# Pinning TensorE's whole order: attention steps placed by counted MLP columns, scores in one burst over four banks, full-height transposes

## The chip, the cores and the metric

The kernel runs on one core of one Trainium2 chip. The core has five engines with instruction queues of their own: TensorE (PE, matrix products), VectorE (DVE), ScalarE (ACT), GpSimd (POOL) and SyncE (SP, which issues most DMAs). The metric is the device time of one launch in microseconds (us), as the median of several runs.

## What is computed

Windowed attention with a linear bias for 8 batches of 8 heads, then a gated MLP on its output. Cut to what matters (here `B, H, S, D = 8, 8, 576, 64`, `d_model` 512, `d_ff` 1024):

```python
scores = q @ k.T / sqrt(D)                       # per batch and head
mask = (rel >= 0) & (rel < 128)                  # rel = query - key position
scores = where(mask, scores - slope[h] * abs(rel), -1e9)
attn = softmax(scores);  x = attn @ v            # heads side by side: [B, S, 512]
h = gelu_tanh(x @ w_in);  u, v = h[..., :512], h[..., 512:]
v_n = (v - mean(v)) / sqrt(var(v) + 1e-6) * g_ln
v_s = einsum('ts,bsd->btd', w_sg, v_n) + b_sg[None, :, None]
out = x + (u * v_s) @ w_out
```

## The kernel before

Attention is done for pairs of heads: 32 pairs, four to a batch, pair n in batch n // 4. A pair goes through steps with one-letter names (the table `STEPS`). Queries and keys come transposed, so that the window of 128 keys is met by blocks of 64 queries against 192 keys. The scores of a pair come in two parts, `a` (`scores(0)`, 12 matmuls with the first block's short ones) and `c` (`scores(2)`, 8 matmuls), each into two banks of PSUM of the pool ps_s, which has two. VectorE adds the bias and takes the minima of the negated scores (`A`, `C`), which also writes the tiles `e` and `e0` to SBUF and so frees the banks; `n` copies the minima to `nb`. ScalarE takes the exponentials (`E`, eight 128x128 tiles and two 64x64 of `e0`, L363), VectorE the inverses of the sums (`R`), and GpSimd scales (`r`, `s`, `S`). PE transposes the four tiles of a head (`t`, `T`, L388) and the small first block (`z`, L401: a 64-row `e0` against a 64x64 identity) into banks of ps_a, which also has two; VectorE masks them on the way out into `px` (`X`, `Y`), ScalarE copies the small block into `p0` (`P`, L404). The step `v` multiplies with the values: one matmul `x2` from `p0` (L421) and 18 into `x1` from `px` (L418). ScalarE gathers both into `xf` (`x`), and `h`, `l`, `k` split it for the MLP into a high and a low half `xs`.

The MLP of a batch (`mlp_block`) runs in parts: a tail of v (L517, L519), two v parts of two 128-row tiles (`v_sum`, L489 to L491, 12 matmuls of 512 columns for each tile), four u parts (L466 to L468, 24 matmuls of 288 columns), four y parts (L551 to L555, 28 of 288 columns) and four output parts (L466 to L468 again, 24 of 288). fp32 is carried as high and low halves, so that three matmuls stand for one product. Each part fills one of the two double banks of ps_m; ScalarE's gelu (L509, L524) and the norm, which goes over VectorE, GpSimd and ScalarE and back, follow a v part, and the results `vn`, `vA`, `vB` are read by y.

The order. The first five pairs are written out by hand in the string `START`, on all engines, with the decoding of the 64-bit weights between; tokens are a step and a pair (`v4`), and `w` tokens are v_sums of the first batch. From the sixth pair on (`FIRST = 5`) the code is issued by a small plan (`PLAN`, `PLAN0`): digits advance a pair to a stage of `STAGES`, letters the pair before, and `m` emits the next MLP part whole. That fixes dependencies and priorities; the order on each engine is then made by the scheduler, which works with modelled times. `burst` keeps the matmuls of a step one behind the other as far as `issue_after` holds them.

A "tail" below is the v tail of a batch, from its L517. There is one in each batch.

Of the kernel before, what the change touches and what calls it, by code (L numbers as in the profile page):

```python
# [21 lines left out]
def attention_gmlp(  # L22
# [17 lines left out]
    nc = tc.nc  # L40
# [244 lines left out]
    class Pair:  # L285
# [25 lines left out]
        def scores(self, t2):  # L311
            qk, heads = self.qk, self.heads
            W = 3 * R
            if t2 == 0:
                self.pr = [att.tile([P, T, P], F32, name="e", bufs=4) for _ in range(2)]
                self.e0 = att.tile([R, 2 * R], F32, name="e0", bufs=2)
            banks = self.banks[t2] = [ps_s.tile([P, 512], F32, name="ps_s") for _ in range(2)]
# [17 lines left out]
            burst(insts)  # L335
# [5 lines left out]
        def minima(self, t2):  # L341
            W = 3 * R
            banks, pr, nm = self.banks.pop(t2), self.pr, self.nm
            for j in range(2):
# [6 lines left out]
                if t2 == 0:  # L351
                    self.shift(h, self.e0[:, j * R:(j + 1) * R], banks[j][0:R, 2 * W:2 * W + R], biases[h][0:R, 2, :], nm[0:R, 2 * T + j:2 * T + j + 1])
# [7 lines left out]
        def exps(self, ts, first=True):  # L360
            def exp(x, i):
                n = x.shape[0]
                nc.scalar.activation(x, x, AF.Exp, bias=self.nm[0:n, i:i + 1], scale=-1.0, accum_out=self.sm[0:n, i:i + 1])  # L363

            for j in range(2):
                for t in ts:
                    exp(self.pr[j][:, t, :], j * T + t)
            for j in range(2 if first else 0):
                exp(self.e0[:, j * R:(j + 1) * R], 2 * T + j)
# [10 lines left out]
        def scale_first(self):  # L380
            self.scaled(self.e0.rearrange("p (m c) -> p m c", m=2), 2 * T)
# [17 lines left out]
        def transpose_first(self):  # L399
            self.ct0 = ps_a.tile([P, 512], F32, name="ps_a")  # L400
            nc.tensor.transpose(self.ct0[:, 0:R], self.e0, ident[0:R, 0:R])  # L401
# [4 lines left out]
        def values(self):  # L406
            vt, px, heads = self.vt, self.px, self.heads
            x1 = self.x1 = ps_a.tile([P, 512], F32, name="ps_a")
            x2 = self.x2 = ps_a.tile([P, 512], F32, name="ps_a")
# [11 lines left out]
            burst([lambda: nc.tensor.matmul(x2[:, 0:R], self.vd, self.p0, start=True, stop=True), *(part(half, t, j) for half, t in order for j in (1, 0))])  # L421
# [18 lines left out]
        def low_tail(self):  # L440
# [11 lines left out]
            "T": lambda p: p.transpose(1), "Y": lambda p: p.masked(1), "v": values, "x": gather, "h": high, "l": low, "k": low_tail,  # L452
        }
        STAGES = ["qL", "aA", "cC", "n", "ER", "rstXzP", "STY", "vx", "hlk"]


    def mm3(dsts, pairs, outer=True):
        if not outer:
            for k in range(len(dsts)):
                mm3(dsts[k:k + 1], [(a, bs[k:k + 1]) for a, bs in pairs])  # L460
            return
# [31 lines left out]
    def v_sums(t2, xs):  # L493
        pv = ps_m.tile([P, 2, 512], F32, name="ps_m")
        for i in range(2):
            v_sum(pv, t2, i, xs, range(NC))
        return pv

    def mlp_block(b, xs, xfs):
# [6 lines left out]
        def v_part(t2):  # L506
            pv = started.pop(t2) if b == 0 and t2 in started else v_sums(t2, xs)
            vg = mlp.tile([P, 2, F], F32, name="vg", bufs=1)
            nc.scalar.activation(vg, pv, AF.Gelu_apprx_tanh)  # L509
            for i in range(2):  # L510
                norm(vg[:, i, :], P, vn[:, 0, t2 + i, :], vn[:, 1, t2 + i, :])

        def v_tail():
# [11 lines left out]
            norm(vg, R, vA[0:R], vA[R:2 * R], vB[0:R])  # L525

        def u_part(f):
            fs = slice(f * P, (f + 1) * P)
            pu = ps_m.tile([P, 2, 512], F32, name="ps_m")
            mm3([pu[:, i, 0:S2] for i in range(2)], [((wi[:, 0, c, fs], wi[:, 1, c, fs]), [(hi_of(xs[c])[:, ss], lo_of(xs[c])[:, ss]) for ss in halves]) for c in range(NC)], U_OUTER)  # L530
            nc.scalar.copy(in2(u4[:, f, :]), pu[:, :, 0:S2])
            us.append(u4[:, f, :])
            if f == NF - 1:
                nc.scalar.activation(u4, u4, AF.Gelu_apprx_tanh)

# [3 lines left out]
        for part, i in FIRST_ORDER if b == 0 else IN_ORDER:  # L539
            {"v": v_part, "t": lambda _: v_tail(), "u": u_part}[part](i)  # L540
            yield
        for f in range(NF):
# [5 lines left out]
            for i, ss in enumerate(halves):  # L548
# [6 lines left out]
                nc.tensor.matmul(y, vB[:, fs], wsB[:, ss], start=False, stop=True)  # L555
            nc.vector.tensor_tensor(in2(u), py[:, :, 0:S2], in2(u), ALU.mult)
            split(g[:, 0, :], g[:, 1, :], u)
            yield
        for c in range(NC):
# [3 lines left out]
            mm3([po[:, i, 0:S2] for i in range(2)], [((wo[:, 0, f, cs], wo[:, 1, f, cs]), [(gs[f][:, 0, ss], gs[f][:, 1, ss]) for ss in halves]) for f in range(NF)], O_OUTER)  # L563
            nc.vector.tensor_tensor(in2(o), po[:, :, 0:S2], in2(o), ALU.add)  # L564
            nc.sync.dma_start(out[b, cs, :], o)
            yield
# [3 lines left out]
    U_OUTER = 0  # L570
    O_OUTER = 1
    LAG = 2
# [7 lines left out]
    done = [0] * len(pairs)  # L580
    mlps = (b for b in range(B) for _ in mlp_block(b, xss[b], xfs[b]))
    parts = 0
# [7 lines left out]
        e1 r0 i5 s0 C1 z0 t0 S0 q3 +0 X0 a2 H1 i3 P0 -1 d5 T0 Y0 i4 -2 H0 f1 A2 v0 -0 L2 x0 R1 c2 m5 e2 r1 b5  # L590
        z1 C2 s1 q4 S1 t1 X1 a3 P1 f2 o5 T1 +5 Y1 h0 R2 d4 v1 A3 s2 l0 x1 L3 H5 t2 m4 k0 w10 b4 e3 X2 -5 w20
        c3 o4 w00 r2 C3 +4 z2 w30 P2 h1 S2 f3 a4 l1 T2 Y2 w31 H4 R3 k1 v2 -4 d3 A4 w01 r3 L4 x2 s3 w11 h2 m3
        t3 S3 e4 z3 X3 w21 l2 c4 T3 b3 w02 o3 k2 w32 Y3 P3 +3 d6 w12 C4 v3 H3 i7 -3 w22 x3 m6 h3 b6 f4 l3 o6
        w13 k3 +6 R4 w23 d7 w03 r4 H6 w33 m7 s4 z4 P4 b7 t4 S4 X4 -6 T4 o7 Y4 +7 v4 H7 -7 x4 h4 l4 k4
# [3 lines left out]
    wchunks = {}  # L598

# [14 lines left out]
    for token in START.split():  # L614
        before = len(nc.cur_bb.bb.instructions)
        start_step(token[0], int(token[1:]))
        for i in nc.cur_bb.bb.instructions[before:]:
            if i.engine in last:
                tc.add_manual_dep(i, last[i.engine], mybir.DependencyInfo(mybir.DependencyClass.NoSync, mybir.DependencyReason.DATA), reason="start")
            last[i.engine] = i.name  # L620
    for n in range(FIRST):
        done[n] = len(Pair.STAGES)

# [3 lines left out]
    PLAN = ['L1fmmg2hm34mi', '1mm2gh3m4Lm5i', 'def1Lgmmmhm2i', 'def1gmmhiLm2m']  # L627
    PLAN0 = {5: '1mLm2m34', 6: 'f1mgL2hm34mi', 7: 'f1mgL2hm34mi', 8: 'f1mgL2hm34mi', 9: '1mm2gh3m4Lm5i'}

    def advance(n, stage):  # L630
        if 0 <= n < len(pairs):
            while done[n] <= stage:
                for op in Pair.STAGES[done[n]]:
                    Pair.STEPS[op](pairs[n])
                done[n] += 1

    nc.sync.dma_start(gb, g_ln.rearrange("(o f) -> o f", o=1).broadcast_to([P, F]))
    steps = decode()
    vec.steps = steps
    for n in range(FIRST, len(pairs) + 1):  # L640
        advance(n, 0)
        for op in PLAN0[n] if n in PLAN0 else PLAN[n % NPAIR]:
            if op == "m":
                if parts < max((n - LAG) // NPAIR, 1) * (len(IN_ORDER) + NF + NC):
                    next(mlps)
                    parts += 1
            elif op == "L":
                advance(n + 1, 0)
            elif op.isdigit():
                advance(n, int(op))  # L650
            else:
                advance(n - 1, ord(op) - ord("a"))
        if n == LAST:
            vec.steps = None
            for _ in steps:
                pass
    for _ in mlps:
        pass
# [25 lines left out]
```

## Time and profile before

| what | us |
|---|---|
| median of three runs | 677.32 |
| lowest and highest | 675.35, 680.73 |
| the profiled execution | 675.89 |
| its span (first to last instruction) | 674.2 |

The granted clock of TensorE was .983 of full speed over the profiled span. A row of the order of time has the start in us, the duration, the engine, the line, the operation, the tiles it writes and reads, the shape and how many records it joins; in square brackets how long the engine idled before, and what ended that. An fp32 matmul leaves two records, so that the 12 score matmuls of the first part read `x24` and the 8 of the second `x16`. PE's durations overlap, since its matmuls are pipelined: what one costs is read from the starts of two that follow each other, not from its own duration.

### The profile page before, as it was taken

The numbers are of one execution on the slowest core, as the hardware profiler recorded it, in microseconds if no ns is written. First come the engines' busy times: TensorE is split into PE (matmuls) and PEld (weight loads), VectorE is DVE, ScalarE is ACT, GpSimd is POOL, SyncE is SP. The second block draws the span as 40 slices with busy tenths as digits, with TensorE's granted clock in tenths as the row PEclk, the third lists the DMA queues.
The fourth block names the chain that finished last, engine by engine and source line by source line (L and its number), as shares of the span: only waits on it lengthen the run. The fifth ranks groups of instructions, "written<-read, shape, count | busy, mean of one in ns | idle before, by whom it ended". The sixth has DMA issues, their size and how long they took to land.

```text
span 674.2 us, 14921 instructions
## 1 busy us (share of the span) xinstructions
PE 638.0 (95%) x5664; PEld 562.6 (83%) x5664; DVE 417.2 (62%) x1372; ACT 334.1 (50%) x979; POOL 244.2 (36%) x241
## 2 busy tenths in 40 slices
PE   3788796999999999999999999999999999999997
PEld 2666585887898889888899889889799888999997
DVE  5887996556646665655576656646576657553511
ACT  7676776434574326633645336742645345731420
POOL 1786657332134322551324321453226321360120
PEclk9998797999999999999999999999999999999999
DMA  8648330233212312224122322133221331001001
GB/s 273 209 128 241 114 125 8 74 106 111 72 48 80 112 53 73 73 74 143 57 59 69 107 73 73 41 103 116 69 59 56 108 106 36 1 2 71 0 1 71
DMA packets 55931, 57.24 MB, mean 85 GB/s; under 512 B 8498, under 2 KB 45362, under 8 KB 55860
## 3 DMA queue, kind: packets, MB, share of 16 engines
q1 hardware_dynamic: 55860, 56.28, 26.7%
q8 instruction: 45, 0.74, 0.5%
q14 instruction: 26, 0.21, 0.1%
HBM read 46.83 MB, written 9.44 MB: 83 GB/s over the span
## 4 chain that ended last, share of the span: by engine, by line
PE 75%; DVE 13%; ACT 7%; DMA 2%; issue 2%; POOL 1%; ACTq 0%; DVEq 0%; POOLq 0%
PE ps_m L466 9%; PE ps_m L467 8%; PE ps_m L468 8%; PE ps_s L320 7%; PE ps_a L418 7%; PE ps_m L551 5%; PE ps_m L552 5%; PE ps_m L553 5%; PE ps_a L388 4%; PE ps_m L489 3%; PE ps_m L490 3%; PE ps_m L491 3%; ACT e L363 3%; DVE vn L482 2%; DVE px L260 2%; DVE st L474 2%
## 5 line engine op out<-in xcount | busy, mean ns | idle before, releaser
L378 POOL TENSOR_TENSOR e<-e,rr 128x512 f32<-128x512 f32 (+1 forms) x96 | 77.9, 833 | 170.7 <-DVE rr L260 140.9
L363 ACT ACTIVATE e<-e,nb 128x128 f32<-128x128 f32 x270 | 101.7, 378 | 28.8 <-DVE nb L260 28.7
L320 PE MATMUL ps_s<-qk 64*64 64x192 f32 (+2 forms) x1280 | 79.7, 326 | 12.3 <-DMA qk<-qkT 8.0
L466 PE MATMUL ps_m<-xs,wi 128*128 128x288 f32 x256 | 79.2, 309 | 0.9 <-ACT vg L509 0.5
L551 PE MATMUL ps_m<-ws,vn 128*128 128x288 f32 x256 | 79.1, 309 | 0.0
L466 PE MATMUL ps_m<-g,wo 128*128 128x288 f32 x256 | 77.9, 305 | 0.2 <-DVE xf L564 0.2
L477 POOL TENSOR_TENSOR rs<-rs,mhalf 128x1 f32<-128x1 f32 (+1 forms) x40 | 35.3, 893 | 116.2 <-DVE rs L476 116.2
L552 PE MATMUL ps_m<-ws,vn 128*128 128x288 f32 x256 | 77.1, 301 | 0.0
L468 PE MATMUL ps_m<-xs,wi 128*128 128x288 f32 x256 | 76.9, 300 | 0.0
L553 PE MATMUL ps_m<-ws,vn 128*128 128x288 f32 x256 | 76.8, 300 | 0.0
L467 PE MATMUL ps_m<-g,wo 128*128 128x288 f32 x256 | 76.7, 301 | 0.0
L467 PE MATMUL ps_m<-xs,wi 128*128 128x288 f32 x256 | 76.6, 299 | 0.0
L320 PEld LDWEIGHTS ps_s<-qk 64*64 64x64 f32 x1280 | 50.2, 141 | 31.0 <-issue 18.9
L468 PE MATMUL ps_m<-g,wo 128*128 128x288 f32 x256 | 75.7, 297 | 0.0
L251 POOL TENSOR_TENSOR g<-u,g 128x576 fp32r<-128x576 f32 x32 | 45.4, 1419 | 68.3 <-ACT g L250 62.8
L418 PE MATMUL ps_a<-px,vt 128*64 128x128 f32 (+1 forms) x1152 | 64.4, 267 | 4.6 <-issue 2.8
L418 PEld LDWEIGHTS ps_a<-px,vt 128*64 128x64 f32 x1152 | 59.3, 142 | 10.3 <-issue 8.9
L260 DVE CUSTOM_DVE_ANT_0 e<-ps_s,bias 128x128 f32<-128x128 f32 (+1 forms) x256 | 57.1, 265 | 0.4
L260 DVE TENSOR_TENSOR px<-ps_a,m_old 128x512 f32<-128x512 f32 x64 | 43.8, 685 | 19.8 <-PE ps_a L388 19.5
L489 PE MATMUL ps_m<-wi,xs 128*128 128x512 f32 x128 | 52.5, 410 | 2.4 <-ACT xs L433 2.4
L438 POOL TENSOR_TENSOR xs<-xf,xs 128x576 fp32r<-128x576 f32 x32 | 46.4, 1461 | 21.1 <-DVE xs L260 20.9
L551 PEld LDWEIGHTS ps_m<-ws,vn 128*128 128x128 f32 x256 | 49.2, 192 | 3.7 <-issue 2.2
(113 smaller groups left out, 1487.6 us busy)
## 6 DMA issues: line engine op xcount, KB each, us to landing
qk<-qkT SPq DMA_DIRECT2D x32, 576.0 KB, 3.9
vt<-v_in SPq DMA_DIRECT2D x64, 256.0 KB, 3.2
outT<-xf SPq DMA_DIRECT2D x32, 288.0 KB, 2.1
wst<-w_in SPq DMA_DIRECT2D x8, 512.0 KB, 7.2
vt<-v_in SPq DMA_DIRECT2D x64, 32.0 KB, 2.9
wst<-w_out SPq DMA_DIRECT2D x4, 512.0 KB, 3.9
wst<-w_sgT SPq DMA_DIRECT2D x4, 288.0 KB, 4.1
vd<-v_in SPq DMA_DIRECT2D x64, 16.0 KB, 2.1
```

Source lines behind the costliest of these rows:

```text
L260: inst = getattr(nc.vector, name)(*args, **kw)
L320: return lambda: nc.tensor.matmul(dst, qk[js, 0, q0:q0 + R], qk[js, 1, k0:k1], start=True, stop=True)
L363: nc.scalar.activation(x, x, AF.Exp, bias=self.nm[0:n, i:i + 1], scale=-1.0, accum_out=self.sm[0:n, i:i + 1])
L378: nc.gpsimd.tensor_tensor(x, x, self.rr[0:n, i:i + m].rearrange("p (m o) -> p m o", o=1).broadcast_to([n, m, c]), ALU.mult)
L418: return lambda: nc.tensor.matmul(x1[heads[j], q0 + lo // 2 * R if t < 0 else q0 + t * R:q0 + (hi + 1) // 2 * R], block, px[j][:, (half * ...
L466: nc.tensor.matmul(dst, ah, bh, start=(i == 0), stop=False)
L467: nc.tensor.matmul(dst, ah, bl, start=False, stop=False)
L468: nc.tensor.matmul(dst, al, bh, start=False, stop=(i == n - 1))
L489: nc.tensor.matmul(pv[:, i, :], xh, wi[:, 0, c, F:], start=(c == 0), stop=False)
L551: nc.tensor.matmul(y, vn[:, 0, t, fs], ws[:, 0, t, ss], start=(t == 0), stop=False)
L552: nc.tensor.matmul(y, vn[:, 0, t, fs], ws[:, 1, t, ss], start=False, stop=False)
L553: nc.tensor.matmul(y, vn[:, 1, t, fs], ws[:, 0, t, ss], start=False, stop=False)
```

## The change

From the sixth pair on PE's order is written out whole: each PE instruction depends on the one issued ahead of it (`in_order`), and the scheduler orders the other engines around it. `PLAN` is now a list of places: a pair begins at a multiple of `FULL`, the MLP's columns per pair (29,056), and its steps come at given fractions of that, when so many MLP columns have gone by. `mlp_block` yields after each half part how many columns it has issued. Besides:

- Both parts of a pair's scores (`*`) are one burst of 20 matmuls; the first goes to ps_a, the second to ps_s.
- `e0` is one of two constant 128x128 tiles, zeroed once; its transpose takes all 128 rows.
- `x2` is a step of its own, `2` in START and `3` in the plan (`values_first`); in the plan it stands behind the second transposes (`TY3`), and `V` behind it holds the 18 others. Both are in ps_s there.
- `mm3` works one half at a time everywhere, also in the output parts, which used to do both halves per weight.
- `LAST` is 7: the rest of the weights' decoding is flushed one pair later.

```diff
+    e0s = []
+    for i in range(2):
+        x = const.tile([P, 2 * R], F32, name=f"e0_{i}")
+        nc.gpsimd.memset(x, 0.0)
+        e0s.append(x)
...
-        def scores(self, t2):
+        def scores(self, *t2s):
+            insts = [x for t2 in t2s for x in self.score_list(t2, ps_a if len(t2s) > 1 and t2 == 0 else ps_s)]
+            burst(insts)
...
-            nc.tensor.transpose(self.ct0[:, 0:R], self.e0, ident[0:R, 0:R])
+            nc.tensor.transpose(self.ct0[:, 0:P], self.e0, ident)
...
+        def values_first(self, pool):
+            self.x2 = pool.tile([P, 512], F32, name=pool.name)
+            nc.tensor.matmul(self.x2[:, 0:R], self.vd, self.p0, start=True, stop=True)
...
-            burst([lambda: nc.tensor.matmul(x2[:, 0:R], self.vd, self.p0, start=True, stop=True), *(part(half, t, j) for half, t in order for j in (1, 0))])
+            burst([part(half, t, j) for half, t in order for j in (1, 0)])
...
-        STAGES = ["qL", "aA", "cC", "n", "ER", "rstXzP", "STY", "vx", "hlk"]
+        STEPS["*"] = lambda p: p.scores(0, 2)
+        STEPS["3"] = lambda p: p.values_first(ps_s)
+        STEPS["V"] = lambda p: p.values(ps_s)
...
-    LAST = 6
+    LAST = 7
...
-        w13 k3 +6 R4 w23 d7 w03 r4 H6 w33 m7 s4 z4 P4 b7 t4 S4 X4 -6 T4 o7 Y4 +7 v4 H7 -7 x4 h4 l4 k4
+        w13 k3 +6 R4 w23 d7 w03 r4 H6 w33 m7 s4 z4 P4 b7 t4 S4 X4 -6 T4 o7 Y4 +7 24 v4 H7 -7 x4 h4 l4 k4
...
+    def in_order(engines=None):
+
+        before = len(nc.cur_bb.bb.instructions)
+        yield
+        for i in nc.cur_bb.bb.instructions[before:]:
+            if engines is None or i.engine in engines:
+                if i.engine in last:
+                    tc.add_manual_dep(i, last[i.engine], mybir.DependencyInfo(mybir.DependencyClass.NoSync, mybir.DependencyReason.DATA), reason="in_order")
+                last[i.engine] = i.name
...
-    PLAN = ['L1fmmg2hm34mi', '1mm2gh3m4Lm5i', 'def1Lgmmmhm2i', 'def1gmmhiLm2m']
+    BEGINS = [0, 0.95, 1.7, 2.4, 3.0, 3.6, 4.4]
+    PLAN = [(0.0, "*ACnq"), (0.45, "ER"), (0.8, "rsS"), (1.25, "tzXP"), (1.4, "TY3"), (1.7, "VxhlkL")]
```

What that makes of the order is shown at three places. The first is ScalarE around the tail of a batch. The rows are the copy of the small first block into p0 (`COPY p_...`, L404 before, L414 after), the tables' loads, the gelus of the tail (L524, L539) and of a v part (L509, L523), and the exps (L363, L373). Before:

```order
L404 COPY p_1_127<-ps_a 128x64
L524 ACT_TABLE_LOAD
L524 ACTIVATE vg<-vg 64x512
L363 ACT_TABLE_LOAD
L363 ACTIVATE e,stats_135<-e,nb 128x128 x8
L363 ACTIVATE e_5585,stats_135<-e_5585,nb 64x64
L479 ACTIVATE vA<-vg,rs 64x512
L481 ACTIVATE vB<-vg,rs 64x512
L363 ACTIVATE e_5585,stats_135<-e_5585,nb 64x64
L509 ACT_TABLE_LOAD
L509 ACTIVATE vg<-ps_m 128x1024
```

After:

```order
L539 ACT_TABLE_LOAD
L539 ACTIVATE vg<-vg 64x512
L491 ACTIVATE vA<-vg,rs 64x512
L493 ACTIVATE vB<-vg,rs 64x512
L373 ACT_TABLE_LOAD
L373 ACTIVATE e,stats_135<-e,nb 128x128 x5
L523 ACT_TABLE_LOAD
L523 ACTIVATE vg<-ps_m 128x1024
L373 ACT_TABLE_LOAD
L373 ACTIVATE e,stats_135<-e,nb 128x128 x3
L414 COPY p_2_130<-ps_a 128x64
```

The copy of p0 stood ahead of the tail's gelu and now stands behind the next pair's eight exps, which a v part's gelu parts in two.

The second place is PE in the same v parts (L501 to L503 after, L489 to L491 before, are v_sum's matmuls). Before, at the end of the tail, and then around x2 (L421), 49 rows later:

```order
L388 MATMUL ps_a<-ident,e 128x128 x4
L401 MATMUL ps_a<-ident,e_5376 128x64
L517 MATMUL ps_m<-wi,xs 128x512 x4
L519 MATMUL ps_m<-wi,xs 64x512 x4
L320 MATMUL ps_s<-qk 64x192 x8
L388 MATMUL ps_a<-ident,e 128x128 x4
```

```order
L489 MATMUL ps_m<-wi,xs 128x512
L490 MATMUL ps_m<-wi,xs 128x512
L491 MATMUL ps_m<-wi,xs 128x512
L421 MATMUL ps_a<-p_1_127,vd_125 128x64
L418 MATMUL ps_a<-px,vt 64x64 x2
L418 MATMUL ps_a<-px,vt 64x128 x12
L418 MATMUL ps_a<-px,vt 64x64 x4
```

After, x2 (L418 now) in the middle of the second v part; the values (L431) follow twelve matmuls later:

```order
L501 MATMUL ps_m<-wi,xs 128x512
L502 MATMUL ps_m<-wi,xs 128x512
L503 MATMUL ps_m<-wi,xs 128x512
L398 MATMUL ps_a<-ident,e 128x128 x4
L418 MATMUL ps_s<-p_2_130,vd_128 128x64
L501 MATMUL ps_m<-wi,xs 128x512
L502 MATMUL ps_m<-wi,xs 128x512
L503 MATMUL ps_m<-wi,xs 128x512
```

The matmul that reads p0 was 48 MLP matmuls behind the transposes and is now directly behind them, with twelve MLP matmuls between the two transposes' groups.

The third place is PE at the end of START, around the scores of pair 5 (L320, L330). Before:

```order
L320 MATMUL ps_s<-qk 64x192 x6
L320 MATMUL ps_s<-qk 64x64 x2
L489 MATMUL ps_m<-wi,xs 128x512
L490 MATMUL ps_m<-wi,xs 128x512
L320 MATMUL ps_s<-qk 64x192 x8
L491 MATMUL ps_m<-wi,xs 128x512
L489 MATMUL ps_m<-wi,xs 128x512
L490 MATMUL ps_m<-wi,xs 128x512
```

Seven more such matmuls follow, and then the small transpose of pair 4. After:

```order
L411 MATMUL ps_a<-ident,e_0_131 128x128
L398 MATMUL ps_a<-ident,e 128x128 x8
L418 MATMUL ps_a<-p_1_127,vd_125 128x64
L431 MATMUL ps_a<-px,vt 64x64 x2
L431 MATMUL ps_a<-px,vt 64x128 x12
L431 MATMUL ps_a<-px,vt 64x64 x4
L330 MATMUL ps_a<-qk 64x64
L330 MATMUL ps_a<-qk 64x128
L330 MATMUL ps_a<-qk 64x64
L330 MATMUL ps_a<-qk 64x128
L330 MATMUL ps_a<-qk 64x192 x6
```

The scores of pair 5 stood among v_sum matmuls, ahead of pair 4's transposes; now they stand behind pair 4's transposes and values (its x2 is `p_1_127`), and the v_sum matmuls stand ahead of all of that.

More of the change, by code (lines that the diff above doesn't have):

```diff
@@ L539, in mlp_block @@
         for part, i in FIRST_ORDER if b == 0 else IN_ORDER:
-            {"v": v_part, "t": lambda _: v_tail(), "u": u_part}[part](i)
-            yield
+            yield from {"v": v_part, "t": lambda _: v_tail(), "u": u_part}[part](i)
         for f in range(NF):
```

146 lines of the change are left out of this document (75 added, 71 removed).

## The prediction

> **What bounds the kernel now.** I read the page's busy times first, then a table of windows, then the waits of TensorE, then its order of time. The page's first lines:
>
> ```profile
> span 674.2 us, 14921 instructions
> PE 638.0 (95%) x5664; PEld 562.6 (83%) x5664; DVE 417.2 (62%) x1372; ACT 334.1 (50%) x979; POOL 244.2 (36%) x241
> ```
>
> TensorE (PE) leads, but a share is an average, so the stretches come next; the columns are busy time of each engine and, third from the end, PE's granted clock:
>
> ```profile
> 58.90:61.30 2.40, 0.04 (x3) 0.01 (x1) 1.66 (x14) 1.46 (x5) 1.59 (x2) 1.00 1.08 294
> 61.30:64.70 3.40, 3.40 (x20) 1.97 (x21) 1.50 (x6) 2.11 (x10) 3.40 (x3) 0.50 0.67 180
> 64.70:74.90 10.20, 6.89 (x54) 5.03 (x52) 10.12 (x21) 9.44 (x27) 6.39 (x8) 1.00 0.43 141
> 104.50:111.10 6.60, 0.07 (x2) 0.01 (x1) 5.87 (x6) 6.57 (x14) 5.57 (x6) 0.85 0.00 0
> 111.10:115.90 4.80, 4.80 (x20) 4.80 (x21) 2.05 (x9) 1.25 (x2) 2.42 (x2) 0.50 0.00 0
> 115.90:616.00 500.10, 498.64 (x4536) 443.13 (x4536) 304.87 (x1040) 237.90 (x716) 163.88 (x160) 1.00 0.24 74
> ```
>
> From 115.9 to 616 us PE is busy 498.6 of 500.1 us at full clock: it waits for nobody, so each microsecond taken from its work there counts, and each new wait counts just as much. In the dense stretch ahead of it, where attention, the first MLP and the weights' decoding meet, VectorE (DVE) is full (10.12 of 10.20 us) and sets the pace. And an idle PE pays twice: after 2.4 us without work it ran 3.4 us at half clock, after 6.6 us it ran 4.8.
>
> **What the change takes from PE.** The price of a burst is the time from its first row's start to the next MLP matmul, with what MLP matmuls in its place would add:
>
> ```profile
> 302.28 0.30 PE L467 MATMUL ps_m<-g,wo 128*128 128x288 f32 x1
> ...
> 303.76 0.29 PE L466 MATMUL ps_m<-g,wo 128*128 128x288 f32 x1
> 303.89 0.60 PE L388 MATMUL ps_a<-ident,e 128*128 128x128 f32 x4
> 304.42 0.27 PE L401 MATMUL ps_a<-ident,e 64*128 64x64 f32 x1
> 304.62 0.88 PE L320 MATMUL ps_s<-qk 64*64 64x192 f32 x16
> 305.43 0.40 PE L467 MATMUL ps_m<-g,wo 128*128 128x288 f32 x1
> 305.67 0.29 PE L468 MATMUL ps_m<-g,wo 128*128 128x288 f32 x1
> ```
>
> Eleven steps of 288 columns take 303.76 − 302.28 = 1.48 us, .1345 each. A burst of four transposes is 4 × .11 = .44 when another transpose follows; here .53, since the small transpose from 64 rows enters late (.09), holds .20 and leaves late too: about .40 in all. As a full-height 128-row transpose it is one more of the .11: .29 saved per pair. The first MLP matmul behind a scores burst steps .24 instead of .1345, .105 lost at each exit. Before, a pair's scores are two bursts:
>
> ```profile
> 461.29 0.60 PE L388 MATMUL ps_a<-ident,e 128*128 128x128 f32 x4
> 461.73 0.33 PE L421 MATMUL ps_a<-p,vd 128*128 128x64 f32 x2
> 461.99 1.00 PE L320 MATMUL ps_s<-qk 64*64 64x64 f32 x24
> 462.92 0.40 PE L466 MATMUL ps_m<-g,wo 128*128 128x288 f32 x1
> ...
> 466.31 1.88 PE L418 MATMUL ps_a<-px,vt 128*64 128x64 f32 x36
> 468.12 0.40 PE L466 MATMUL ps_m<-g,wo 128*128 128x288 f32 x1
> ```
>
> The 24 records of the first cost .93, .105 at the exit and .09 at the entry, 1.12; the 16 of the second .81 + .105 + .09, 1.0. In one burst one exit, one entry and a change of banks, again about .09, fall away: 1.84, .28 saved. These two give .57 a pair. The values take 1.81 + .19 = 2.0, x2 some .22 (.26 above, part of it the scores' entry). So a pair's attention before, unsplit, is 2 × .44 + .40 + .22 + 1.12 + 1.0 + 2.0 = 5.62, and 5.05 after. The scheduler also cut bursts before, an entry and an exit each time; the pinned order has none of that. What the cuts cost, from the starts of two v_tail groups (L517), four batches apart:
>
> ```profile
> 240.00 1.21 PE L517 MATMUL ps_m<-wi,xs 128*128 128x512 f32 x4
> 548.02 0.97 PE L517 MATMUL ps_m<-wi,xs 128*128 128x512 f32 x3
> 402.65 0.40 PE L490 MATMUL ps_m<-wi,xs 128*128 128x512 f32 x1
> ...
> 404.99 0.39 PE L491 MATMUL ps_m<-wi,xs 128*128 128x512 f32 x1
> ```
>
> 308.02 / 4 = 77.0 us a batch. A 512-column step is 2.34 / 10 = .234, so the MLP takes 304 × .134 + 56 × .234 = 53.8; the rest, 23.2, is four pairs at 5.8, .2 of it cuts. Together .77 a pair, times the 26 pairs that are planned among MLP columns: **−20 us** (bounds −15, the two counted savings alone, and −23).
>
> **What the change makes PE wait for.** In the order of the changed kernel the step `2` (x2, L418) stands right behind the second transposes, inside the batch's v parts (v_sum, t2 = 2 and 0, called v2 and v0 here), and no longer ahead of the values. `2` reads p0, copied by ScalarE (ACT), whose new order puts that copy behind five exps, a gelu and three exps of the *next* pair, with three table loads. All PE work behind `2` is held. Before, the copy came at once, ahead of the batch's tail, and its reader 14 us later:
>
> ```profile
> 472.26 0.21 ACT L404 COPY p<-ps_a 128x64 f32<-128x64 f32 x1 [3.44 <-PE ps_a L401]
> 478.93 1.28 ACT L363 ACT_TABLE_LOAD   x1 [2.54 <-DVE nb L260]
> 480.23 0.40 ACT L363 ACTIVATE e<-e,nb 128x128 f32<-128x128 f32 x1
> ...
> 483.33 0.33 ACT L363 ACTIVATE e<-e,nb 64x64 f32<-64x64 f32 x1
> 486.63 1.02 ACT L509 ACTIVATE vg<-ps_m 128x1024 f32<-128x1024 f32 x1
> 486.71 0.33 PE L421 MATMUL ps_a<-p,vd 128*128 128x64 f32 x2
> 478.69 0.15 DVE L260 COPY nb<-stats 128x10 f32<-128x10 f32 x1
> 419.27 1.00 PE L320 MATMUL ps_s<-qk 64*64 64x64 f32 x24
> 420.30 0.50 DVE L260 COPY_PREDICATED ps_s<-sel,ps_s 128x128 f32<-128x128 uint8 x2 [2.56 <-PE ps_s L320]
> 393.72 0.49 DVE L260 COPY_PREDICATED ps_s<-sel,ps_s 128x128 f32<-128x128 uint8 x2 [2.24 <-PE ps_s L320]
> ...
> 395.25 0.68 DVE L260 TENSOR_TENSOR px<-ps_a,m_old 128x512 f32<-128x512 f32 x1
> 479.08 0.73 DVE L478 SCALAR_TENSOR_TENSOR vg<-vg,mv,gb 64x512 f32<-64x512 f32 x1
> ```
>
> The walk, with 0 at the end of a tail. PE: v2's first half, 12 × .234, to 2.8; scores to 4.65; second half to 7.45; transposes .44 + .11 to 8.0; v0's first half to 10.8; transposes to **11.25**, where `2` is due. DVE: minima of the first scores begin 420.30 − 419.27 = 1.03 after the burst's start, at 3.85, take 395.25 − 393.72 = 1.53; the tail's last operation lies between, .73 (as the row of L478); the second minima, with two 64x64 operations fewer, some 1.4; so nb is begun at 7.5. ACT: a load starts 478.93 − 478.69 = .24 later and takes 1.3, to 9.05; eight exps took 483.33 − 480.23 = 3.1, .3875 each, so five end at 11.0; load 1.3 and gelu 1.0 to 13.3; load to 14.6; three exps and the copy (1.16 + .21) to **16.0**. PE stands 4.7 us (4.0 if DVE's tail operation slips behind, 5.5 if ACT's vA copies come between). The next pair's `2` is due 7.6 after its scores start; nb comes after 4.1, ten exps end 3.8 and a copy of u .6 later, P's copy .2: 8.7, a wait of 1.1, and the third pair's some .5 by the same sum with more columns between. 6.3 a batch, in the five batches where a tail, v parts and scores meet: **+31 us** (bounds +20, the `2` alone at 4.0; +40).
>
> **The clock.** The rows 58.9 and 104.5 above put half clock behind 2.4 and 6.6 us of idleness. 4.7 lies between them. 3.4 us at .50 hold 1.7 us of full-speed work, so five stalls cost **+8.5** (0 if none is followed so, 12 with the 4.8 us). The Trainium skill, "TensorE: Matmul & The Clock Gate", Part 1, has the clock fall only after at least one idle window of about 3.4 us that runs free: by it a 4.7-us stall would be caught in one case of three, +2.8 instead, and the sum 5.7 lower. This trace's 2.4-us gap disagrees with it, and I go by the trace.
>
> **The dense stretch to 116 us.** DVE is full there, so cheaper PE work brings nothing. At the end of the hand order the 15 v_sum matmuls that stood around pair 5's scores, while DVE and ACT worked on pair 4, now stand ahead, and pair 4's transposes, values and pair 5's scores follow bare: 15 × .234 = 3.5 of cover lost. Both transposes of pairs 7 and 9 come without MLP between them, and the second needs the bank that masking must read first, 1.33 (two of the .67): 3.0 with the handovers. The `2`s there wait behind up to eight exps, 3.1. Waits for banks:
>
> ```profile
> PE ps_m L554 <- DVE vA L482: 6.5, 1, 6.5
> PE ps_s L320 <- DVE stats L260: 3.5, 3, 2.0
> ```
>
> With four banks wanted at once I double the 3.5. In return the 6.5 for vA shrinks to 1.3, since later MLP leaves DVE time, and its half clock (2.4) goes: −7.6. Sum 3.5 + 3.0 + 3.1 + 3.5 − 7.6 = **+5.5** (−6 if only the return happens, +14 if it doesn't). Zeroing e0 once on POOL and the MLP groups cut into halves cost nothing: POOL is busy 36%, and the matmuls stay. LAST 7 spreads the same weight work over one pair more. On SP's queue the loads of the next pair move behind other steps, but a pair lasts 77.0 / 4 = 19 us and qk lands in 3.9:
>
> ```profile
> qk<-qkT SPq DMA_DIRECT2D x32, 576.0 KB, 3.9
> ```
>
> **Sum.** 675.9 (the profiled run, 1.7 more than its span) − 20 + 31 + 8.5 + 5.5 = 700.9. The median of the three runs is 677.3, 1.4 above; so **702 us**.
>
> **Rivals.** (A) Faster: ACT's copy of p0 is served in time and `2` holds nothing; the whole saving stays, with the dense stretch: 675.9 − 20 + 5.5 + 1.4 = 663. For it speaks that PE is the bound. Against it: from the scores' start to `2` PE has 8.4 us, and ACT's work after nb alone is eight exps, three loads and a gelu, 3.1 + 3.9 + 1.0 = 8.0, with nb itself 4.7 after the scores' start. It decides if all waits a batch come to less than (20 − 5.5) / 5 = 2.9 us. Chance .12. (B) No change: the `2` alone waits, 4.7 × 5 = 23, the clock stays, and the dense stretch is even: 675.9 − 20 + 23 + 1.4 = 680; .14. (C) Worse: a second stall in each batch halves the clock too, 702 + 8.5 = 710, and the dense stretch costs its +14 as well, 719; 715 for the two in part; .16. My forecast, 691 to 711, .58. That the order would not be what the plan says is excluded: the order shows it pinned.
>
> **Chances and range.** About 1% is what a measurement of this kernel can tell from no change, 670.5 to 684.1. Faster: A and .01 of B, .13. Same: .12 of B. Slower: the last .01 of B, my case and C, .75. The range leaves out A and the top of C: 674 to 717.
>
> **What would show it.** Right: a row of PE at `2` (L418 of the changed kernel) some 4 to 5 us long released by ACT's p0 copy, five times, between tails about 80 us apart; windows behind it at .50 clock; scores as one group of 40 without MLP between; between stalls, pairs that cost 5.05. If the tails are 74 us apart, A holds and my walk on ACT is wrong; if stalls stand but the clock stays 1.00, the clock term is. The tail at 240.00 has the dense stretch and some nine cheaper pairs before it, and should come at 240 + 5.5 − 7 = 239; much earlier, and the dense term has the wrong sign.

## The result

The changed kernel takes 716.23 us (median of 4 runs, 715.63 to 717.41), the kernel before 676.34 beside it: ratio 1.058, 95% interval 1.053 to 1.064. It is slower by 40 us. The profiled execution took 715.63, its span is 713.9. The first lines of its page:

```profile
span 713.9 us, 14846 instructions
PE 625.7 (88%) x5664; PEld 563.9 (79%) x5664; DVE 416.8 (58%) x1372; ACT 357.1 (50%) x997; POOL 246.6 (35%) x243
```

PE does the same 5664 records in 12 us less busy time, and the span is 40 us longer: what was saved on PE's work was lost several times over in waits. ScalarE has 18 records more, the tables' loads around exps that a gelu now parts in two. The view of PE's waits names them (total in us, times, longest):

```profile
PE ps_s L418 <- ACT p L414: 35.4, 17, 5.0
PE ps_s L330 <- DMA qk<-qkT: 7.6, 2, 5.3
PE ps_m L532 <- ACT u L550: 5.3, 1, 5.3
PE ps_a L398 <- DVE stats L266: 4.8, 2, 4.3
...
PE ps_m L501 <- ACT xs L446: 3.8, 1, 3.8
PE ps_s L330 <- DVE stats L266: 3.5, 3, 2.0
...
PE ps_a L411 <- DVE stats L266: 2.5, 2, 1.5
...
PE ps_m L573 <- DVE vA L494: 1.1, 1, 1.1
```

The first row didn't exist before: x2 waits for ScalarE's copy of p0, 35.4 us in all. The wait for vA, 6.5 before, has come down to 1.1, as forecast; but a new one of 5.3 for ScalarE's u (L532) stands ahead of the first tail, at 98 us, with half clock behind it. One of the long waits, in the order of time (start, duration, engine, line, operation; in brackets the idle time ahead):

```profile
261.41 0.60 PE L398 MATMUL ps_a<-ident,e 128*128 128x128 f32 x4
261.98 1.28 ACT L523 ACT_TABLE_LOAD   x1
263.27 1.02 ACT L523 ACTIVATE vg<-ps_m 128x1024 f32<-128x1024 f32 x1
264.32 1.28 ACT L373 ACT_TABLE_LOAD   x1
265.61 0.40 ACT L373 ACTIVATE e<-e,nb 128x128 f32<-128x128 f32 x1
...
266.78 0.19 ACT L414 COPY p<-ps_a 128x64 f32<-128x64 f32 x1
267.02 0.69 PE L418 MATMUL ps_s<-p,vd 128*128 128x64 f32 x2 [5.01 <-ACT p L414]
...
331.47 1.20 PE L532 MATMUL ps_m<-wi,xs 128*128 128x512 f32 x4
...
579.94 1.20 PE L532 MATMUL ps_m<-wi,xs 128*128 128x512 f32 x4
```

The transposes end at 262.0 and PE has nothing else that it may do: ScalarE loads the gelu's table, runs the gelu, loads the exps' table, runs three exps, and then the copy, which could have run since the small transpose at 258.5. From the two tails (L532), three batches apart, a batch takes (579.94 − 331.47) / 3 = 82.8 us, where it was 77.0. The windows around that wait (busy time of PE, its weight loads, DVE, ACT, POOL; then the clock), and below them the end of the dense stretch:

```profile
248.70:262.00 13.30, 13.30 (x97) 10.17 (x93) 8.09 (x34) 7.18 (x17) 0.99 (x1) 1.00 0.37 111
262.00:267.00 5.00, 0.01 (x1) 0.00 (x0) 2.67 (x8) 4.96 (x11) 0.00 (x0) 0.79 0.00 0
267.00:271.70 4.70, 4.68 (x12) 3.81 (x13) 4.36 (x7) 2.30 (x7) 4.62 (x5) 0.50 0.03 7
271.70:331.50 59.80, 58.51 (x605) 55.47 (x604) 34.02 (x120) 28.44 (x85) 20.41 (x20) 1.00 0.26 78
...
81.00:109.00 28.00, 21.56 (x196) 19.29 (x196) 17.03 (x64) 17.91 (x42) 7.84 (x8) 0.94 0.32 102
```

The same 28 us of the kernel before:

```profile
81.00:109.00 28.00, 23.48 (x192) 20.51 (x192) 26.59 (x57) 21.25 (x49) 18.14 (x16) 0.93 0.34 103
```

Two things are seen. The wait of 5.0 us is followed by 4.7 us at half clock. And between 81 and 109 us VectorE, which was full before (26.59 of 28), works 17.03: it starves.

### The profile page after: what moved, and what is told of

It reads as the page before. It is cut to its first block, busy times and chain, and to the rows that moved or that the text cites. A ratio compares the mean times of both kernels' runs of the same rounds, so it can differ in the third digit from the quotient of the medians.

```text
span 713.9 us, 14846 instructions
## 1 busy us (share of the span) xinstructions
PE 625.7 (88%) x5664; PEld 563.9 (79%) x5664; DVE 416.8 (58%) x1372; ACT 357.1 (50%) x997; POOL 246.6 (35%) x243
## 4 chain that ended last, share of the span: by engine, by line
PE 47%; DVE 22%; ACT 20%; POOL 4%; issue 4%; DMA 2%; SPq 1%; POOLq 0%; ACTq 0%; DVEq 0%
ACT e L373 10%; PE ps_m L478 7%; PE ps_m L479 6%; PE ps_m L480 6%; DVE e L266 6%; PE ps_s L431 5%; PE ps_m L570 3%; PE ps_m L571 3%; PE ps_m L572 3%; DVE st L486 2%; DVE vn L494 2%; ACT L373 2%; ACT L523 2%; PE ps_a L330 2%; POOL rs L489 2%
## 5 line engine op out<-in xcount | busy, mean ns | idle before, releaser
L373 ACT ACTIVATE e<-e,nb 128x128 f32<-128x128 f32 x270 | 101.9, 379 | 75.9 <-DVE nb L266 75.7
L388 POOL TENSOR_TENSOR e<-e,rr 128x512 f32<-128x512 f32 (+1 forms) x96 | 80.1, 857 | 140.3 <-DVE rr L266 71.3
L489 POOL TENSOR_TENSOR rs<-rs,mhalf 128x1 f32<-128x1 f32 (+1 forms) x40 | 35.9, 909 | 171.7 <-DVE rs L488 171.7
L478 PE MATMUL ps_m<-xs,wi 128*128 128x288 f32 x256 | 78.1, 305 | 0.0
L479 PE MATMUL ps_m<-xs,wi 128*128 128x288 f32 x256 | 75.7, 296 | 0.0
L480 PE MATMUL ps_m<-xs,wi 128*128 128x288 f32 x256 | 75.6, 295 | 0.0
L501 PE MATMUL ps_m<-wi,xs 128*128 128x512 f32 x128 | 58.1, 454 | 3.8 <-ACT xs L446 3.8
L503 PE MATMUL ps_m<-wi,xs 128*128 128x512 f32 x128 | 54.8, 428 | 1.3 <-POOL xs L451 1.3
L502 PE MATMUL ps_m<-wi,xs 128*128 128x512 f32 x128 | 54.6, 426 | 0.0
L486 DVE BATCH_NORM_STATS2 st<-vg 128x6 f32<-128x512 f32 (+1 forms) x40 | 26.1, 685 | 45.9 <-ACT vg L523 38.1
L431 PEld LDWEIGHTS ps_s<-px,vt 128*64 128x64 f32 x972 | 47.0, 137 | 5.9 <-issue 5.3
L256 ACT ACTIVATE g<-u 128x576 fp32r<-128x576 f32 x32 | 21.9, 683 | 59.5 <-DVE u L577 59.5
```

The source lines that it names most:

```text
L388: nc.gpsimd.tensor_tensor(x, x, self.rr[0:n, i:i + m].rearrange("p (m o) -> p m o", o=1).broadcast_to([n, m, c]), ALU.mult)
L431: return lambda: nc.tensor.matmul(x1[heads[j], q0 + lo // 2 * R if t < 0 else q0 + t * R:q0 + (hi + 1) // 2 * R], block, px[j][:, (half * ...
L478: nc.tensor.matmul(dst, ah, bh, start=(i == 0), stop=False)
L479: nc.tensor.matmul(dst, ah, bl, start=False, stop=False)
L480: nc.tensor.matmul(dst, al, bh, start=False, stop=(i == n - 1))
L501: nc.tensor.matmul(pv[:, i, :], xh, wi[:, 0, c, F:], start=(c == 0), stop=False)
```

## The experiments

Each run stands beside runs of the kernel before on the same chip (medians 675.9 to 676.8). Ratios are to that kernel, with 95% intervals.

**e1_x2_late**: x2 back beside the value matmuls.

```diff
-    PLAN = [..., (1.4, "TY3"), (1.7, "VxhlkL")]
+    PLAN = [..., (1.4, "TY"), (1.7, "3VxhlkL")]
```

> The changed kernel, with one thing undone: x2 stands with the 18 other value matmuls again, no longer right behind the second transposes. Theory (PE is held at x2 by ScalarE's copy of p0, which stands behind eight exps and a gelu): the 35.4 us of waits for that copy fall to under 4, and with them the half clock behind the five long ones (about 11 us); the tails of batches 2 to 6, 82.7 us apart, come 74 to 76 apart; 670 to 680 us. Rival (the copy is only where PE's lateness shows; the next reader of ScalarE's or VectorE's work, the value matmuls or the next scores' banks, waits instead): most of the 35 us reappears under another name, 700 to 716 us.

Measured: 691.12 us, ratio 1.018 [1.012, 1.025]. Its view of waits:

```profile
PE ps_s L418 <- ACT p L414: 11.1, 5, 2.2
```

The time lies between the two ranges expected. (The traced execution took 685.11, the other three 691.1 to 692.2.) The waits for the copy fell from 35.4 to 11.1, not under 4: five of 2.2 us are left, since ScalarE's order is what it was and the copy comes so late that even the later place is too early. A batch is 77.5 us (tails at 398.9 and 476.4). The theory holds in kind; in size it took the later place for enough.

**e2_copy_first**: PE's order as changed; each exp gets an order dependency on the copy of p0 of the pair before.

```diff
-                nc.scalar.activation(x, x, AF.Exp, ...)
+                inst = nc.scalar.activation(x, x, AF.Exp, ...)
+                if self.n > FIRST:
+                    tc.add_manual_dep(inst.ins, pairs[self.n - 1].copied, ..., reason="copy_first")
```

> The changed kernel, PE's order untouched, x2 right behind the second transposes; only on ScalarE the exps of a pair are put behind the copy of p0 of the pair before. Theory (the copy's place on ScalarE is the whole cause): the copy comes right after the small transpose, before the exps can start anyway; waits of x2 under 3 us in all, tails 74 to 76 us apart, 668 to 680 us. Rival (order of PE is too tight in itself): the exps, scaled tiles and transposes of the next pair come later by what the copy gains, PE waits at the transposes, 690 to 716 us.

Measured: 674.63 us, ratio .9965 [.994, .999]. The same place as above in its order of time, and its windows over four batches and over the dense stretch:

```profile
321.33 1.20 PE L534 MATMUL ps_m<-wi,xs 128*128 128x512 f32 x4
...
334.02 0.60 PE L400 MATMUL ps_a<-ident,e 128*128 128x128 f32 x4
334.45 0.33 PE L420 MATMUL ps_s<-p,vd 128*128 128x64 f32 x2
...
331.84 0.20 ACT L416 COPY p<-ps_a 128x64 f32<-128x64 f32 x1
332.06 1.28 ACT L373 ACT_TABLE_LOAD   x1
333.36 0.41 ACT L373 ACTIVATE e<-e,nb 128x128 f32<-128x128 f32 x1
...
396.33 0.50 PE L534 MATMUL ps_m<-wi,xs 128*128 128x512 f32 x1
```

```profile
81.00:109.00 28.00, 21.60 (x196) 19.31 (x196) 16.86 (x64) 17.84 (x42) 7.83 (x8) 0.94 0.32 102
...
246.30:546.30 300.00, 296.63 (x2836) 270.76 (x2832) 197.96 (x668) 159.84 (x464) 102.50 (x100) 1.00 0.27 82
```

The copy is done at 332.0, x2 follows the transposes without a gap at 334.45, PE is busy 296.6 of 300.0 us and a batch takes 75.0 (321.33 to 396.33). One order on ScalarE is worth 716.23 − 674.63 = 41.6 us. Nothing came late in its place. The dependency does a second thing: the eight exps stay in one piece, and 10 of ScalarE's 50 table loads fall away. The dense stretch didn't move: VectorE still works 16.86 of 28.

**e3_scores5**: pair 5's scores and minima into the hand order, ahead of pair 4's transposes.

```diff
-        w13 k3 +6 R4 w23 d7 w03 r4 H6 w33 m7 s4 z4 ...
+        w13 k3 +6 a5 R4 w23 d7 A5 w03 r4 H6 c5 w33 m7 s4 C5 n5 z4 ...
```

> The changed kernel; the scores and minima of pair 5 go back among the v_sum matmuls of the hand order, ahead of pair 4's transposes, where they stood before. x2's place is as changed. Theory (the lost cover at the end of the hand order made pairs 5 to 8 some 20 us late, and costs 10 to 15 us): 700 to 707 us, the first two tails 5 to 10 us earlier than in the changed kernel (98.1 and 165.9). Rival (VectorE is full in that stretch, so the order of PE's work there moves nothing): 714 to 718 us, tails where they were.

Measured: 717.34 us, ratio 1.060 [1.055, 1.064], with the tail of the first batch at 94.4 instead of 98.1, of the second at 169.2 instead of 165.9. What pair 5 gained was lost one pair on. In the view of waits two have grown (3.9 and 1.1 in the change):

```profile
PE ps_a L398 <- ACT p L414: 9.8, 3, 5.0
...
PE ps_m L479 <- POOL g L257: 5.4, 3, 2.7
```

By its numbers the rival had it, but its reason (VectorE is full) is refuted by the windows above. The run moves only one of the late pairs: pair 6's scores still began at 98 us, against 67 in the kernel before.

**e4_warm**: 32 unread matmuls ahead of x2 in the five long waits; they change no output.

```diff
+            if self.n > 12 and self.n % 4 == 1:
+                for _ in range(32):
+                    nc.tensor.matmul(self.x2[:, R:R + 288], wi[:, 0, 0, 0:P], wi[:, 0, 0, 0:288], start=True, stop=True)
```

> The changed kernel with 32 matmuls of 288 columns that nothing reads put ahead of x2 in the five long stalls (about 4.3 us of 5.0 each), so that PE isn't idle there. Nothing else is changed, x2 still waits for ScalarE. Theory (idle PE loses the clock, and each long stall costs 1.5 to 3 us afterwards): no half clock behind the five places, 703 to 709 us. Rival (half clock behind the stalls costs nothing, since what follows waits for other engines anyway, or the clock falls all the same): 714 to 719 us.

Measured: 721.44 us, ratio 1.065 [1.059, 1.071], slower than the change itself. Windows of one batch:

```profile
262.00:268.00 6.00, 5.19 (x40) 4.94 (x39) 3.06 (x8) 5.94 (x17) 0.31 (x1) 1.00 0.00 0
284.00:289.50 5.50, 2.89 (x23) 2.64 (x22) 2.18 (x5) 4.57 (x22) 1.14 (x2) 1.00 0.00 0
289.50:292.90 3.40, 3.40 (x16) 3.40 (x15) 1.63 (x2) 0.00 (x0) 2.60 (x3) 0.50 0.06 14
```

The clock stayed at 1.00 behind the filled wait, but PE then came sooner to the next pair's x2 and waited 2.6 us there instead of 1.0, and lost the clock behind that one. Half clock after the long wait had cost little: it had only used up time that the next wait would have taken.

**e5_fullz_alone**: the kernel before with the full-height transposes alone.

```diff
-                self.e0 = att.tile([R, 2 * R], F32, name="e0", bufs=2)
+                self.e0 = e0s[self.n % 2]
...
-            nc.tensor.transpose(self.ct0[:, 0:R], self.e0, ident[0:R, 0:R])
+            nc.tensor.transpose(self.ct0[:, 0:P], self.e0, ident)
```

> The kernel before with one part of the change alone: the small first block is kept in a zeroed 128x128 tile and transposed at full height. Theory (the 64-row transpose costs .40 us of PE, .29 more than a full-height one, in each of the 27 pairs that PE is the bound for): 676.8 - 7.8, 667 to 671 us, and a row of transposes followed at once by MLP matmuls 11 to .13 apart. Rival (the entry and exit of the transposes cost the same whatever their height, or ScalarE's copy of the block is what is waited for): 675 to 678 us.

Measured: 678.82 us, ratio 1.004 [1.002, 1.006]: the theory's 7.8 us did not come. In its order of time (L394 transposes, L407 the small one, L326 scores):

```profile
347.41 0.66 PE L394 MATMUL ps_a<-ident,e 128*128 128x128 f32 x4
347.90 0.27 PE L407 MATMUL ps_a<-ident,e 128*128 128x128 f32 x1
348.10 0.54 PE L326 MATMUL ps_s<-qk 64*64 64x192 f32 x4
...
364.27 0.54 PE L326 MATMUL ps_s<-qk 64*64 64x192 f32 x2
364.74 0.66 PE L394 MATMUL ps_a<-ident,e 128*128 128x128 f32 x4
365.32 0.88 PE L326 MATMUL ps_s<-qk 64*64 64x192 f32 x14
```

The transpose itself is cheaper: where an MLP matmul follows, .137 us pass from the start of the last of the four transposes ahead of it to that matmul, against .405 in the kernel before. But the order that the scheduler made is another: scores of 16 records are cut into 12 and 4, or 2 and 14 around transposes. Over three batches the score bursts stood in 39 pieces, before in 31; from start to next start PE spent 8.9 us of a batch on scores, before 8.0, and a batch took 78.6 us instead of 77.0. A saving on PE is kept only where its order is kept.

**e6_burst_alone**: the kernel before with the four-bank burst alone, from pair 5 on; the values of these pairs go to ps_s with it.

```diff
-        STAGES = ["qL", "aA", "cC", "n", ...]
+        STEPS["*"] = lambda p: p.scores(0, 2)
+        STAGES = ["qL", "*A", "C", "n", ...]
```

> The kernel before with another part alone: from the sixth pair on both parts of the scores in one burst over four banks (two of ps_a, two of ps_s), values in ps_s; PE's order is left to the scheduler. Theory (one entry, one exit and a change of banks saved, .28 us a pair, and the cuts of the second burst gone): 665 to 671 us. Rival (scores in ps_a keep transposes waiting until VectorE has read them, and VectorE is late in the dense stretch): 677 to 700 us, new waits of the transposes for VectorE's stats.

Measured: 686.88 us, ratio 1.016 [1.012, 1.020], as the rival has it, though the waits are not those it named: batches 3 to 6 take 76.7 us, .3 less than before, and the 10 us are lost ahead of them. Its window of the dense stretch:

```profile
81.00:109.00 28.00, 22.85 (x164) 20.32 (x157) 17.51 (x55) 19.75 (x44) 9.18 (x9) 0.86 0.25 80
```

VectorE starves here just as in the change, with nothing pinned: pair 5's scores began at 80.6 us. In the kernel before they began at 57.9, in the change at 81.2.

**e7_unpinned**: e2_copy_first, PE free until pair 9 begins (the loop over events is run without `in_order` up to `begin(9)`).

> The kernel of e2_copy_first (copy of p0 ahead of the next exps), with PE's order left to the scheduler until pair 9 begins, and pinned from there on. Theory A (the fixed order is what makes the stretch from 58 to 165 us slow): tails of the first two batches at 93 to 95 and 155 to 160 instead of 98.2 and 164.3, 664 to 670 us. Theory B (pair 5's scores are late because their first part needs both banks of ps_a, which pair 4's transposes and values hold until about 79 us, whatever the order): pair 5's scores stay near 80 us, 672 to 677 us.

Measured: 669.92 us (665.57 to 673.57), ratio .989 [.983, .995]: by the time, the upper edge of theory A's range. Pair 5's scores began at 86.2, the first two tails stood at 97.3 and 161.0; some 5 us of each are a stretch at half clock in the profiled run (last section). Without it pair 5 is still late with PE's order free, as theory B has it, but the tails, at some 92 and 156, are near A's. So both have a part. The fixed order of these pairs costs 4.7 us by the medians (674.63 − 669.92), a size that isn't well known: the intervals of the two ratios touch.

**e8_hybrid**: e2_copy_first with pairs 5 to 8 by the plan of the kernel before (two score parts in ps_s, PE free), the pinned plan from pair 9 on. `LAST` is 6 again.

```diff
+    PINNED = 9
...
+    STAGES = ["qL", "aA", "cC", "n", "ER", "rstXzP", "STY", "2vx", "hlk"]
...
+    for n in range(FIRST, PINNED):
+        advance(n, 0)
+        for op in PLAN0[n]:
...
+    def begin(n):
+        return (n - PINNED - 0.04) * FULL
```

> The kernel of e2_copy_first with pairs 5 to 8 issued by the plan of the kernel before, scores in two parts in ps_s and PE's order left to the scheduler; from pair 9 on the pinned plan, four-bank scores, copy of p0 ahead of the next exps. Full-height transposes throughout. Theory (what the change loses before 240 us is that pairs 5 and 6 come 23 and 36 us later and VectorE starves): scores of pair 5 near 58 us again, tails of batches 1 and 2 at 93 and 158, the third at 235 to 240 instead of 246.3, then 75.0 a batch; 664 to 669 us. Rival (VectorE is full in that stretch and sets its length, so what comes when on PE there matters little): 673 to 677 us.

Measured: 661.15 us, ratio .978 [.9755, .980]: faster than both kernels, and below the range of its theory. Two windows of it, and a burst of scores:

```profile
32.20:45.90 13.70, 11.07 (x130) 8.51 (x129) 11.41 (x43) 10.79 (x44) 10.55 (x9) 1.00 0.52 156
...
81.00:109.00 28.00, 21.61 (x191) 18.89 (x190) 26.60 (x57) 21.24 (x49) 18.75 (x17) 0.98 0.34 101
```

```profile
256.03 0.94 PE L330 MATMUL ps_a<-qk 64*64 64x64 f32 x22
...
257.61 0.40 PE L480 MATMUL ps_m<-xs,wi 128*128 128x288 f32 x1
257.85 0.29 PE L481 MATMUL ps_m<-xs,wi 128*128 128x288 f32 x1
```

VectorE is full again (26.60 of 28), pair 5's scores begin at 57.0, the first three tails stand at 91.9, 158.0 and 233.0, and a batch takes 75.0 us. The whole burst of scores takes 257.61 − 256.03 = 1.58 and with its exit, .105, and entry some 1.8, as the prediction has it (1.84).

**e9_hybrid_alone**: the same program with the dependency of the exps taken out; PE's order is equal, row for row.

> The kernel of e8_hybrid with ScalarE's order left to the scheduler again, as in the change: PE's order is the same instruction for instruction, the copy of p0 stands behind the next exps. Theory (two causes that add up: late scores before 240 us, worth 13 us, and the copy, worth 42): 716 - 13 = 700 to 705 us, tail of batch 2 at 233 to 236, then 82 to 83 a batch with 5.0-us waits of x2. Rival (early pairs give ScalarE the time it lacks, so that the waits shrink): under 690 us.

Measured: 711.47 us (709.12 to 714.53), ratio 1.051 [1.046, 1.057]. The waits:

```profile
PE ps_s L420 <- ACT p L416: 38.9, 17, 5.0
```

82.8 us a batch, as expected, but the time is in neither range, and the third tail stands at 246.9, not at 233 to 236 (some 5 us of it a stretch at half clock, last section). The early gain is smaller than the 13 us expected, about 5: with the pinned plan from pair 9 on, one more long wait (5.0 us, to 182.6) falls between the second and the third tail, where the change has waits of 2.6. The two causes don't add: the dependency of the exps is worth 711.47 − 661.15 = 50.3 us here, and 41.6 in the change.

**e10_hybrid_late2**: e8_hybrid with x2 back beside the values (the edit of e1).

> The kernel of e8_hybrid with x2 moved back to the other value matmuls; the copy of p0 stays ahead of the exps. Theory (once the copy is served in time the place of x2 on PE costs nothing but its entry): 660 to 663 us. Rival (x2's place is a cost of its own, by the burst that it shortens or by ps_s banks): 655 to 659 or 664 to 670 us.

Measured: 662.54 us, ratio .978 [.974, .982]; a batch is 75.0 us again. With the copy served, x2's place is worth nothing either way.

**e11_warm2**: e4_warm, and 18 more unread matmuls ahead of the next pair's x2.

> The kernel of e4_warm with 18 more unread matmuls ahead of the x2 of the next pair, whose wait had grown from 1.0 to 2.6 us there and was followed by half clock. Both waits of a batch are filled now and the clock should stay at 1.00 from batch 2 to 6. Theory A (half clock costs what it takes from PE's work, 1.6 to 2.3 us a batch): 81 us a batch, 705 to 713 us. Theory B (ScalarE sets the times of both x2, so that PE at full clock only waits longer): 83 to 84 us a batch, 717 to 723 us.

Measured: 716.08 us (712.92 to 719.23), ratio 1.058 [1.052, 1.064]. Windows of one batch:

```profile
255.10:267.00 11.90, 11.90 (x90) 9.22 (x87) 8.10 (x34) 5.79 (x9) 0.98 (x1) 1.00 0.41 123
267.00:274.00 7.00, 6.19 (x45) 5.68 (x44) 3.26 (x8) 6.94 (x22) 0.51 (x1) 1.00 0.01 2
274.00:337.30 63.30, 62.78 (x631) 59.37 (x629) 37.37 (x126) 30.12 (x89) 24.51 (x24) 1.00 0.25 74
```

The clock is 1.00 throughout and the batch takes 82.2 us (255.1 to 337.3): .6 less than the change, neither the 81 of A nor the 83 to 84 of B. ScalarE's order sets the time between two x2; the clock lost behind a wait is mostly time that would have been waited.

**e12_hybrid_banks**: e8_hybrid, but pairs 5 to 8 use the four-bank burst and values in ps_s.

```diff
-    STAGES = ["qL", "aA", "cC", "n", "ER", "rstXzP", "STY", "2vx", "hlk"]
+    STAGES = ["qL", "*A", "C", "n", "ER", "rstXzP", "STY", "3Vx", "hlk"]
```

> The kernel of e8_hybrid, pairs 5 to 8 still issued by the plan of the kernel before with PE's order left to the scheduler; but their scores are one burst over two banks of ps_a and two of ps_s, and their values in ps_s, as from pair 9 on. Theory (banks: pair 5's scores can't start until pair 4's transposes and values have left ps_a): scores of pair 5 near 80 us instead of 57, VectorE busy 17 to 18 of the 28 us from 81 to 109 instead of 26.6, tail of batch 2 at 243 to 248 instead of 233.0, 670 to 678 us. Rival (the pinned order or the new plan's places made those pairs late): 659 to 664 us.

Measured: 676.63 us (672.86 to 679.15), ratio .998 [.994, 1.001]: 15 us above e8_hybrid. Pair 5's scores began at 85.3 instead of 57.0 (some 5 of it again half clock). Its window:

```profile
81.00:109.00 28.00, 22.65 (x171) 20.35 (x172) 15.17 (x55) 17.70 (x41) 9.75 (x10) 0.78 0.32 100
```

The burst over four banks brings the early loss back, with PE's order free. (Five of the ten executions lie at 678.5 to 679.2, the profiled one with the half clock among them; the fastest, 672.9, is 12 us above e8_hybrid's fastest, 660.6.) The run changes the banks and joins the two bursts in one edit. That it is the banks is read from the row that starts pair 5's scores in the changed kernel:

```profile
81.24 0.99 PE L330 MATMUL ps_a<-qk 64*64 64x64 f32 x22 [0.68 <-ACT xf L439]
```

The first part writes to ps_a and was released by ScalarE's gather of pair 4's values out of ps_a. Before, the scores' banks in ps_s were free at 57.9, and the scores went between the v_sum matmuls of the hand order.

## Why the prediction was right, and where its sizes were off

The forecast was 702 us and slower, range 674 to 717; 716.2 came. That it lies inside, by .8 us, is luck: the early stretch lost 11 us more than its term, for a cause that the prediction priced at 3.5 us. Point by point:

- *x2 holds PE for ScalarE's copy, +31 us.* Right in the place, and near in the size. The five long waits are 5.0 us (4.7 was forecast, and up to 5.5), the second of a batch 1.0 to 1.6 (1.1), and with the third's .3 PE idles 6.0 to 6.9 us in each of the five batches (6.3). The walk is .3 us short of each. e2_copy_first shows the cause: the one dependency takes the waits away, and 41.6 us with them. The terms of the forecast that hang on the copy are 31, the clock's 8.5 and the dense stretch's 3.1: 42.6. That they meet the 41.6 is partly luck. With the clock kept (e11_warm2) a batch takes 82.2 us, 7.2 more than the 75.0 of e2_copy_first, so the waits alone are worth some 36 in five batches, more than the 31, and the clock at most 3 of its 8.5.
- *The clock, +8.5 us.* The sign that the prediction named for it came: half clock followed all five long waits, in pieces of 3.4 or 6.8 us, of which 3.1 to 5.8 lay behind the wait. As a term to be added it was still wrong in kind: e11_warm2 keeps the clock and wins .6 us a batch, e4_warm loses .9, because the next wait grows. The Trainium skill's rule ("TensorE: Matmul & The Clock Gate", Part 1: a whole idle window of about 3.4 us) disagrees with the traces here: a wait of 2.6 us in e4_warm was enough, five times of five. The traces don't give a sharp limit in its place: of the five waits of 2.2 us in e1_x2_late three were followed by half clock, the 2.6 us that end at 205 us in the changed kernel were not, and those of 1.0 to 1.6 there were not either.
- *PE's work, −20 us.* The sign is right, the size too large. Without the waits a batch takes 75.0 us instead of 77.0, with .8 to .9 of other waits in it: 2.8 us or .70 a pair of the .77 forecast, and .5 a pair in the end, since the shorter work uncovers waits of .3 to .5 for ScalarE's copies of u and GpSimd's g. e8_hybrid, which pins 23 pairs, is 14.7 us below the kernel before; 7 of these lie ahead of the third tail (233.0 against 240.0), where only four pairs are pinned, and no run splits them. The parts: the burst of scores costs what was forecast, the full-height transpose saves .405 − .137 = .27 (.29). But e5_fullz_alone, without the fixed order, gave all of it back.
- *The dense stretch, +5.5 us.* This step failed, in its premise: "DVE is full there, so cheaper PE work brings nothing", and 3.5 us of lost cover. VectorE is full only as long as PE feeds it. The change sends pair 5's scores to ps_a, where pair 4's transposes and values are until 80 us, and VectorE then works 17.0 us of 28 instead of 26.6. The wait was in the order, and the prediction looked at it as 15 matmuls of cover and at the banks as a doubled 3.5. The waits for VectorE's minima alone (`stats` in the view of waits) came to 3.5 + 4.8 + 2.5 = 10.8 us, not 7.0; and against the 5.4 us by which the wait for vA shrank stands the new one for u, 5.3. The prediction's own test failed here: the third tail, due at 239, came at 248.7. Without the copy's part the forecast for this stretch was 5.5 − 3.1 = 2.4; from e2_copy_first to e8_hybrid it is 674.6 − 661.2 = 13.5. e12_hybrid_banks brings all of it back with the order free. Yet e7_unpinned, with the same banks and a free order but the new plan's places, is 4.7 below e2_copy_first; so what the fixed order has of the 13.5 depends on the plan.

The sum, as a chain of medians: −14.7 (e8_hybrid to the kernel before beside it, 675.9) + 13.5 + 41.6 = 40.4, where 716.2 − 676.3 = 39.9 was measured. That it closes is no proof of the parts, since each step starts where the last one ended; the 50.3 in e9_hybrid_alone shows that in another order they would have other sizes. Against the forecast (−20 + 2.4 + 42.6) the terms of the copy are off by 1, the saving by 5 and the early stretch by 11. The rival that would have made it faster, A, is now a kernel: with the copy served in time e2_copy_first came to 674.6, not 663, again for the early stretch. What stays open: why the free order in e7_unpinned wins its 4.7 us though pair 5 is as late and e12_hybrid_banks, also free, wins nothing, and whether a pinned order for pairs 5 to 8 with scores in ps_s would do as well as the old plan.

## What to carry to other kernels

Where one engine's order is written out and the others are left to a scheduler, each read of the pinned engine needs a look at what stands ahead of its producer on the *other* queue; here one order dependency on ScalarE was worth 42 us or, with other early pairs, 50, and the walk with durations from the old trace found it to within .3 us. A busy engine that is fed by the one you move is not a floor: look up what its input's buffers wait for, and see whether a new user of a pool finds them free. And price a clock loss only where the work behind it is on the path: before the next wait it is nearly free.

## What the runs showed of the hardware

Half clock came in pieces of 3.4 us and multiples (3.4, 6.8, 10.2, 13.7; only the one at a span's end can be shorter), with starts that moved against the work. The largest piece is not tied to an edit: the profiled runs of five kernels (e7 and e9 to e12) have 13.7 us at half clock from 32 us on, the others none of that length there, in the hand order. The profiled run of e10_hybrid_late2, whose hand order is that of e8_hybrid's window above (clock 1.00):

```profile
32.20:45.90 13.70, 11.26 (x84) 9.37 (x88) 9.40 (x35) 6.92 (x27) 6.13 (x6) 0.50 0.34 103
```

That execution took 666.88 us at a mean clock of .971, the other three of the kernel 661.2 to 663.3 at .981 to .986. The spread within the runs of e11_warm2 (712.9 to 719.2) and e12_hybrid_banks (672.9 to 679.2) is about as wide, and their profiled runs, which both had the piece, lie at its upper end.
